# A chunked RWKV-7 recurrence with a SoLU layer behind it: small inverses transposed on VectorE, the first inverse moved, step 6 reordered

## The chip, the cores and the metric

The kernel runs on one core of a Trainium2 chip. The metric is the device time of one execution in microseconds. Before the change it is 708.82 us, the median of three runs (706.29 to 711.25). The profile is of one execution with a span of 705.0 us.

Engines are called PE (TensorE's matmuls; its weight loads are PEld), DVE (VectorE), ACT (ScalarE), POOL (GpSimd) and SP (SyncE, which here only issues transfers). [...]

## The reference

Inputs r, k, v, w, a, b have the shape (4 batches, 8 heads, 768 tokens, 40 channels), fp32. Each head carries a 40x40 state through time:

```
for t in range(768):
    y[t]  = r[t] @ state
    Sa    = state @ a[t]
    state = state * w[t] - outer(Sa, b[t]) + outer(v[t], k[t])
```

The outputs of the 8 heads, side by side, are rows x of 320 values, 3072 rows in all. The second layer computes

```
h    = x @ w_in                     # 320 x 1024
e    = exp(h - max(h)); solu = h * e / (sum(e) + 1e-9)
ln   = (solu - mean) / sqrt(var + 1e-6) * g_ln
out  = ln @ w_out                   # 1024 x 320
```

## The kernel before

**Chunks and steps.** Time is cut into 12 chunks ("rounds") of L = 64 tokens. A step handles one round of two of the four batches, so there are N = 24 steps; steps 2n and 2n+1 belong to round n. Within a chunk the recurrence becomes matrix products, except that the sequential term, the outer product of Sa and b, needs the inverse of a unit triangular 64x64 matrix for each head and batch. This inverse is built from inverses of its 32x32 blocks on the diagonal.

**The parts of a step** are Python generators; each `yield` ends a piece.

- `front(i)`: logarithm of w (lw, L352), its running sums on PE (pcum L356, pcx L369), scaled keys (kx), and the triangular matrix nt (L310). It runs five steps ahead (AHEAD = 5).
- `scatter(n)` writes the diagonal 32x32 blocks of round n to DRAM (blk_dram, L423), and `gather(n)` reads them back with one block to a partition (blk, L433 or L438).
- `invert(n)`: forward substitution on VectorE, one pair of small instructions to a piece. In rounds 0 to 3 (FINE = 4) only the 16x16 blocks are inverted so (L457, L459), in later rounds the whole 32x32 blocks (L492, L494). The result u goes to DRAM, and a transposed copy ut, made by VectorE or ScalarE (L466, L468, L498), goes there as well (L470, L501, L503).
- `bring_inverse(n)` fetches both from DRAM into the layout of the products: tinv from ut_dram (L512, L516) and tinvT from u_dram (L519).
- `solve(i)`: completes the inverses. In fine rounds two products join the 16x16 blocks (py16, y at L619, then pz16); in all rounds two more join the 32x32 blocks (py, pz). All products are groups of 32x32 matmuls at L567.
- Step 0 has no time to invert by substitution and builds its 16x16 inverses by doubling instead (L601 to L615). Each of three levels makes the product with the level's part (py2), y = 1 - product on DVE (L606), then both the new inverse (pz2) and its transpose (pu2) on PE, the one copied by ACT (L612), the other by DVE (L614).
- `attend(i)`, `recurrence(i)` and `readout(i)` are the rest of the attention; pu (L701) is the first product that uses the finished inverse, and x (L682) on DVE goes ahead of it.
- `hidden(m)` and `output(m)`: the second layer, six steps behind (LAG = 6).
- `weights()` fetches w_in and w_out, given as float64, piece by piece over POOL's queue and converts them on DVE and ACT (L178 to L190) during the first six steps. `centre()` (L267, L270) folds the mean of the layer norm into w_out at step 6.

**What sets the order.** Nothing is scheduled by a planner. The order of issue is written by hand as strings, one letter a piece: `turns("f g s ...")`, with EARLY for steps 0 to 5 and STEADY after that. `inverse_steps(i)` says how many pieces of `invert` each letter I runs. All SP transfers share one queue in program order[...]. "*" is a filler matmul without use (L872) that keeps PE active.

Before the change, the first inverse, that of step 1's blocks, runs at the end of the second `turns` (letters I with 2, 4, 4 and the rest), and the loads of rounds 1 and 2 are issued ahead of that `turns`:

```
load(1, "k")
load(1, "v")
load(2, "w")
load(1, "r")
load(2, "a", "b")
turns("f g s f s * g a s f s * f a s g s * g W a s I f s * f a I s a g I s * g f g I W W", ...)
load(2, "k")
scatter(1)
bring_inverse(0, slice(1, 2))
gather(1)
```

Of the kernel before, what the change touches and what calls it, by code (L numbers as in the profile page):

```python
# [64 lines left out]
def kernel(  # L65
# [26 lines left out]

    nc = tc.nc
# [61 lines left out]
    tn_t = const.tile([P, 2, H, 2, Q // 2], FP32, name="tinv")  # L155
# [37 lines left out]
    def weights():  # L193
# [3 lines left out]
        nc.sync.dma_start(out=g_rows, in_=moe_g_ln.rearrange("(c p) -> c p", p=P))  # L197
# [242 lines left out]
    def invert_fine(n):  # L440
# [4 lines left out]
        u = two.tile([P, R, Q], FP32, tag="u", name="u", bufs=1)  # L445
        ut = two.tile([P, R, Q], FP32, tag="ut", name="ut", bufs=1)
        nc.vector.tensor_scalar(out=x, in0=nb, scalar1=-1.0, scalar2=None, op0=ALU.mult)
        nc.vector.memset(x.rearrange("b c t -> b (c t)")[:, 0:R * R:R + 1], 1.0)
        for t in (u, ut):
            for z in range(2):  # L450
                nc.gpsimd.memset(t[half(z)][:, :, R * (1 - z):R * (2 - z)], 0.0)
# [9 lines left out]
        of_round[n]["spilt"] = u.rearrange("b c t -> b (c t)")  # L461
        for key, t, src in (("ut", ut, x.rearrange("b c t -> b t c")), ("u", u, x)):
            dst = of_round[n][key] = dram.tile([64, Q, Q], FP32, tag=key + "_dram", name=key + "_dram")
            for z in range(2):
                if n == 0 and key == "ut":
                    nc.vector.tensor_copy(out=t[half(z)][:, :, R * z:R * z + R], in_=src[half(z)])  # L466
                else:
                    nc.scalar.copy(out=t[half(z)][:, :, R * z:R * z + R], in_=src[half(z)])  # L468
            for z in range(2):
                nc.sync.dma_start(out=dst[:, R * z:R * z + R, :], in_=t[half(z)])  # L470
        yield

    def invert(n):
# [7 lines left out]
        u = two.tile([P, Q // 2, Q], FP32, tag="u", name="u", bufs=1)  # L481
# [15 lines left out]
        ut = two.tile([P, Q, Q // 2], FP32, tag="ut", name="ut", bufs=1)  # L497
        nc.vector.tensor_copy(out=ut, in_=u.rearrange("p c t -> p t c"))  # L498
        ut_dram = of_round[n]["ut"] = dram.tile([P, Q, Q // 2], FP32, tag="ut_dram", name="ut_dram")
        for p in range(2):  # L500
            nc.sync.dma_start(out=u_dram.rearrange("b (c z) t -> b c z t", z=2)[:, :, p], in_=u[half(p)])  # L501
            if p == 0:
                nc.sync.dma_start(out=ut_dram, in_=ut)  # L503
        yield

    def bring_inverse(n, steps=slice(0, 2)):

        ut, u = of_round[n]["ut"], of_round[n]["u"]
        tinv = tn_t[:, steps].rearrange("q s h z c -> q (s h) z c")
        for q in range(4):  # L510
            if n < FINE:
                nc.sync.dma_start(out=tinv[quarter(q)].rearrange("s h z c -> s h (z c)"),  # L512
                                  in_=ut[homes(q, steps)].rearrange("h s t -> s h t"))
            elif q % 2 == 0:
                for p in range(2):
                    nc.sync.dma_start(out=tinv[quarter(q), :, p],  # L516
                                      in_=ut[half(p)][homes(q)].rearrange("h s t -> s h t"))
# [34 lines left out]
    def solve(i):  # L552
# [3 lines left out]
        d["tinvT"], d["tinv"] = ti_t[:, i % 2], tn_t[:, i % 2]  # L556
        nt, tinv, tinvT = given(i, "nt"), d["tinv"], d["tinvT"]
# [16 lines left out]
        def whole(q):  # L574

            return (lambda p, g: nt[quarter(q), p, g, quarter(q % 2)],
                    lambda p, g: tinv[quarter(q), G * p + g].rearrange("s z c -> s (z c)"),
# [9 lines left out]
        if i == 0:  # L587
            tinv_rows, u_rows = tinv.rearrange("q h z c -> q h (z c)"), y_mid.rearrange("q p g c -> q (p g) c")
            unit = c_("one").unsqueeze(1).to_broadcast([P, H, Q])
            y = two.tile([P, H, Q], FP32, tag="u16", name="y", bufs=1)  # L590
# [13 lines left out]
            for j in range(1, 4):  # L604
                t = products("py2", each(level(j), lambda q: whole(q)[1]))
                nc.vector.tensor_tensor(out=y, in0=unit, in1=flat(t), op=ALU.subtract)  # L606
                if j == 1:
                    t = products("pu1", each(lambda q: whole(q)[1], eye))
                    nc.scalar.copy(out=u_rows, in_=flat(t))
# [249 lines left out]
    def inverse_steps(i):  # L859

        if i == 0:
            return [4, 4, 4, 4]
# [122 lines left out]
```

## Time and profile before

| | busy us | share of the span | instructions |
|---|---|---|---|
| PE | 630.7 | 89% | 12873 |
| PEld | 448.6 | 64% | 12873 |
| DVE | 438.4 | 62% | 1188 |
| ACT | 281.2 | 40% | 672 |
| POOL | 121.1 | 17% | 226 |

The shares are means over the whole span. PE counts each fp32 matmul as two records. The profile also slices the span into 40 equal parts and gives the busy share of each engine in a slice as a digit in tenths; PEclk is the clock that PE was granted, and DMA is the mean busy share of the 16 DMA engines. A stage's own limit is read from the slices and from busy time by stage. An entry such as "PE a <- DVE b: 8.2, 4, 3.3" says that PE stood idle ahead of a for 8.2 us in total, four times, 3.3 us the longest, and that DVE's instruction b ended it. "issue" means that the engine waited for nothing that the profile shows. A time line gives start and length of an instruction, and in square brackets the idle time ahead of it with what ended it.

Step 0's first pu (L701) starts at 59.88 us, step 1's at 94.86 us. From about 232 us on, a step takes 23.8 us.

### The profile page before, as it was taken

What the parts mean: (1) busy time and instruction counts of PE and PEld (TensorE: products, weight loads), DVE (VectorE), ACT (ScalarE), POOL (GpSimd) and SP (SyncE); (2) the same over time, 40 slices, a digit from 0 to 9 for tenths busy, and PEclk for the clock granted to TensorE, in tenths of its full rate; (3) what the DMA queues carried; (4) which work ended last, traced back from release to release, by engine and by line L of the source; (5) the groups of instructions that cost most, each with busy time, mean ns of one, the idle gap of its engine ahead of it and who ended that gap; (6) DMA issues with size and microseconds to landing.
All of it is one profiled execution on the core that took longest, in us unless ns stands there. A gap on an engine that the chain in (4) does not pass through costs nothing.

```text
span 705.0 us, 29268 instructions
## 1 busy us (share of the span) xinstructions
PE 630.7 (89%) x12873; PEld 448.6 (64%) x12873; DVE 438.4 (62%) x1188; ACT 281.2 (40%) x672; POOL 121.1 (17%) x226
## 2 busy tenths in 40 slices
PE   7677688898777999999999999999999899979996
PEld 4565566676655767766767676767666666545554
DVE  4116667558487578598697786876986753333442
ACT  3215255455651443444345334534352334312222
POOL 5401341233111112211221122112110100000000
PEclk9869869789997999999999999999999999998999
DMA  9853767568554455554456546554335230000000
GB/s 157 140 93 67 141 122 110 102 120 138 118 108 74 73 88 96 108 90 95 85 78 118 99 84 115 79 103 91 45 71 97 32 58 24 20 24 19 19 17 21
DMA packets 264254, 58.90 MB, mean 84 GB/s; under 512 B 251960, under 2 KB 259904, under 8 KB 264128
## 3 DMA queue, kind: packets, MB, share of 16 engines
q1 hardware_dynamic: 259056, 50.92, 42.6%
q0 software_dynamic: 1664, 5.24, 3.1%
q8 instruction: 101, 1.65, 1.0%
q10 hardware_dynamic: 3408, 0.87, 0.8%
q14 instruction: 25, 0.20, 0.1%
HBM read 38.92 MB, written 13.37 MB: 74 GB/s over the span
## 4 chain that ended last, share of the span: by engine, by line
PE 66%; DVE 15%; ACT 6%; issue 6%; DMA 3%; SPq 2%; ACTq 0%; POOL 0%; DVEq 0%
PE po L813 14%; PE h L768 13%; PE pyo L740 4%; PE plnT L808 4%; PE pcx L369 3%; DVE prod L492 3%; PE py L567 3%; DVE u L494 3%; PE pz L567 3%; PE pcum L356 2%; DVE nmax L778 2%; PE pyo L662 2%; PE plamv L307 2%; PE ppsi L307 2%; PE plamu L307 2%
## 5 line engine op out<-in xcount | busy, mean ns | idle before, releaser
L768 PE MATMUL h<-w_in,xT 128*128 128x512 f32 (+1 forms) x288 | 129.3, 640 | 3.9 <-DVE e L785 3.9
L813 PE MATMUL po<-w,lnT 128*128 128x320 f32 x384 | 115.0, 438 | 0.0
L813 PEld LDWEIGHTS po<-w,lnT 128*128 128x128 f32 x384 | 69.1, 191 | 26.4 <-issue 3.1
L494 DVE TENSOR_TENSOR u<-u,prod 128x30 f32<-128x30 f32 (+7 forms) x240 | 66.1, 275 | 8.2
L492 DVE TENSOR_TENSOR prod<-blk,u 128x30 f32<-128x30 f32 (+7 forms) x240 | 63.9, 266 | 8.2 <-DMA blk<-blk_dram 1.1
L359 POOL TENSOR_TENSOR kx<-raw_b,inv 128x320 f32<-128x320 f32 x24 | 20.8, 866 | 262.3 <-ACT inv L357 185.8
L778 DVE TENSOR_REDUCE nmax<-h 128x1 f32<-128x1024 f32 x24 | 29.3, 1221 | 47.4 <-PE h L768 47.4
L768 PEld LDWEIGHTS h<-w_in,xT 128*128 128x128 f32 (+1 forms) x288 | 38.5, 193 | 31.9 <-issue 30.0
L818 ACT ACTIVATE osb<-po,rs 128x320 f32<-128x320 f32 x24 | 12.7, 528 | 97.1 <-PE po L813 81.4
L747 DVE TENSOR_TENSOR x<-pyo,kx 128x512 f32<-128x512 f32 x24 | 16.6, 691 | 44.8 <-PE pyo L740 44.2
L809 ACT COPY lnT<-plnT 128x512 f32<-128x512 f32 x48 | 27.6, 587 | 35.7 <-PE plnT L808 35.6
L782 ACT ACTIVATE e<-h,nmax 128x1024 f32<-128x1024 f32 x24 | 26.8, 1116 | 35.0 <-DVE nmax L778 35.0
L800 POOL TENSOR_TENSOR rs<-c,mhalf 128x1 f32<-128x1 f32 x24 | 13.2, 550 | 156.7 <-DVE c L799 155.6
L785 DVE TENSOR_TENSOR e<-h,e 128x1024 f32<-128x1024 f32 x24 | 29.4, 1225 | 14.6 <-ACT e L782 14.0
L808 PE MATMUL plnT<-cst,e 128*128 128x128 f32 x192 | 30.5, 289 | 5.7 <-DVE e L785 5.4
L310 DVE TENSOR_TENSOR lamv<-plamv,cst 128x512 f32<-128x512 f32 x24 | 16.6, 691 | 30.3 <-PE plamv L307 30.1
L369 PEld LDWEIGHTS pcx<-cst,lw 128*128 128x128 f32 x192 | 28.2, 202 | 9.7 <-ACT y_mid L646 3.6
L369 PE MATMUL pcx<-cst,lw 128*128 128x132 f32 x192 | 33.3, 301 | 1.1 <-ACT kx L371 0.5
L650 ACT ACTIVATE tinvT<-pz 32x256 f32<-32x256 f32 x48 | 17.9, 374 | 39.9 <-PE pz L567 39.6
L371 ACT ACTIVATE kx<-pcx 128x264 f32<-128x264 f32 x48 | 18.9, 393 | 35.0 <-PE pcx L369 33.0
L808 PEld LDWEIGHTS plnT<-cst,e 128*128 128x128 f32 x192 | 22.9, 146 | 14.2 <-issue 4.3
L726 POOL TENSOR_TENSOR sm<-tot,fac 128x320 f32<-128x320 f32 x20 | 14.7, 736 | 98.2 <-DVE tot L725 71.6
(144 smaller groups left out, 1221.0 us busy)
## 6 DMA issues: line engine op xcount, KB each, us to landing
blk<-blk_dram SPq DMA_DIRECT2D x16, 256.0 KB
raw_k<-in_k_dram SPq DMA_DIRECT2D x24, 160.0 KB
v<-in_v_dram SPq DMA_DIRECT2D x24, 160.0 KB
r<-in_r_dram SPq DMA_DIRECT2D x24, 160.0 KB
out_dram<-osb SPq DMA_DIRECT2D x24, 160.0 KB
raw_w<-in_w_dram SPq DMA_DIRECT2D x23, 160.0 KB
raw_b<-in_b_dram SPq DMA_DIRECT2D x23, 160.0 KB
raw_a<-in_a_dram SPq DMA_DIRECT2D x23, 160.0 KB
```

Source lines behind the costliest of these rows:

```text
L307: nc.tensor.matmul(t[half(c ^ p * cross), p, g * L:(g + 1) * L], lhsT=lhs[half(p), g, half(c)], rhs=rhs[half(p), g, half(c)], start=True, ...
L369: nc.tensor.matmul(t[:, g * 132:g * 132 + 132], lhsT=pair(lw, 2 * j + g), rhs=cst[:, lo:lo + 132], start=True, stop=True)
L492: nc.vector.tensor_tensor(out=t, in0=nb[:, j:j + 1, j + 1:Q].to_broadcast([P, rows, m]), in1=u[:, 0:rows, j:j + 1].to_broadcast([P, rows, ...
L494: nc.vector.tensor_tensor(out=u[:, 0:rows, j + 1:Q], in0=u[:, 0:rows, j + 1:Q], in1=t, op=ALU.subtract)
L567: nc.tensor.matmul(t[quarter(out), c:c + Q], lhsT=lhs(p, g), rhs=rhs(p, g), start=True, stop=True)
L740: nc.tensor.matmul(t[half(p), c, g * W:g * W + used], lhsT=kb[half(c), j, 2 * g + p, :], rhs=lam[half(c), h % 2, h // 2, 0:used], start=i ...
L768: nc.tensor.matmul(h[:, j * 512:j * 512 + 512], lhsT=of_round[i // 2]["xT"][rows, kt, i % 2 * P:i % 2 * P + P], rhs=w_in[rows, 4 if kt == ...
L778: nc.vector.tensor_reduce(out=nmax, in_=h, axis=AX.X, op=ALU.max, negate=True)
L785: nc.vector.tensor_tensor(out=q, in0=h, in1=e, op=ALU.mult)
L808: nc.tensor.transpose(out=t[:, j * P:(j + 1) * P], in_=q[:, f * P:(f + 1) * P], identity=ident)
L809: nc.scalar.copy(out=lnT[:, fs.start:fs.stop].rearrange("p f t -> p (f t)"), in_=t)
L813: nc.tensor.matmul(o[:, 0:DM], lhsT=lnT[:, f, :], rhs=w2[:, f, :], start=f == 0, stop=f == NF - 1)
```

## The change

ut is no longer made, stored and fetched. Instead VectorE transposes tinvT's 32x32 blocks in place of the fetch of tinv: one new piece at the head of `solve(i)` for i > 0, for which the strings EARLY, STEADY and CENTRE have one more "s" right behind the last "r", some pieces ahead of the first product. In step 0 VectorE's transposes take the place of the products pu, pu2 and of half of pz16. The first inverse is spread among step 0's doublings, and the loads of round 2 (w, a, b) and of round 1 (v, r) are issued behind it. Step 6 has an order of its own, and the inversion pieces of the early steps are distributed anew.

```diff
-    tn_t = const.tile([P, 2, H, 2, Q // 2], FP32, name="tinv")
+    tinv = const.tile([P, 2, G, L], FP32, name="tinv")
...
-        nc.sync.dma_start(out=g_rows, in_=moe_g_ln.rearrange("(c p) -> c p", p=P))
+        nc.gpsimd.dma_start(out=g_rows, in_=moe_g_ln.rearrange("(c p) -> c p", p=P))
...
-        u = two.tile([P, R, Q], FP32, tag="u", name="u", bufs=1)
-        ut = two.tile([P, R, Q], FP32, tag="ut", name="ut", bufs=1)
+        u = two.tile([P, R, Q], FP32, tag="u", name="u")
...
-        ut = two.tile([P, Q, Q // 2], FP32, tag="ut", name="ut", bufs=1)
-        nc.vector.tensor_copy(out=ut, in_=u.rearrange("p c t -> p t c"))
-        ut_dram = of_round[n]["ut"] = dram.tile([P, Q, Q // 2], FP32, tag="ut_dram", name="ut_dram")
...
-                nc.sync.dma_start(out=tinv[quarter(q)].rearrange("s h z c -> s h (z c)"),
-                                  in_=ut[homes(q, steps)].rearrange("h s t -> s h t"))
...
             t = products("py1", each(level(0), eye))
-            nc.vector.tensor_tensor(out=tinv_rows, in0=unit, in1=flat(t), op=ALU.subtract)
+            nc.vector.tensor_tensor(out=t_0, in0=unit, in1=flat(t), op=ALU.subtract)
+            nc.vector.transpose(out=u_0, in_=t_0)
             yield
             for j in range(1, 4):
                 t = products("py2", each(level(j), lambda q: whole(q)[1]))
                 nc.vector.tensor_tensor(out=y, in0=unit, in1=flat(t), op=ALU.subtract)
-                if j == 1:
-                    t = products("pu1", each(lambda q: whole(q)[1], eye))
-                    nc.scalar.copy(out=u_rows, in_=flat(t))
                 yield
                 t = products("pz2", each(lambda q: whole(q)[2], grown))
-                nc.scalar.copy(out=tinv_rows, in_=flat(t))
-                t = products("pu2", each(grown, lambda q: whole(q)[2]))
-                nc.vector.tensor_copy(out=u_rows, in_=flat(t))
+                nc.scalar.copy(out=t_0, in_=flat(t))
+                nc.vector.transpose(out=u_0, in_=t_0)
                 yield
+        else:
+            cols = slice(0, L if fine else Q)
+            nc.vector.transpose(out=tinv[:, :, :, cols], in_=tinvT[:, :, :, cols])
+            yield
...
-                         [(q, whole(q)[2], whole(q)[3]) for q in (0, 2)])
+                         [(q, whole(q)[2], whole(q)[3]) for q in (0, 2) if i])
...
-    EARLY = ("r r a r B W f I r r W I W y r X W a s f L W a I a s W f a f W s I a f W s I f W",
-             "r r a r W f r r W g W y r W a f g L W a I a s f g W a I s f g W I s a f g W I s f g W")
-    STEADY = "r b r a r B f b b o r o I o r o y o r X I o h a f L a s a h f a I h f s h f h a f h"
+    EARLY = ("r r a r B W f I r r W I W y r s X W a I s f L W a I a s W f I a f W s I a f W s f W",
+             "r r a r W f r r W g W y r s W a f g L W a I a s f g W a I s f g W I s a f g W I s f g W I")
+    STEADY = "r b r a r B f b b o r o I o r o y o r s X I o h a f L a s a h f a I h f s h f h a f h"
+    CENTRE = "r r a r f o I r o r o y o r s X I o h a f L a s a h I f s a h I f s h f s h I a f h"
...
         if i == 0:
-            return [4, 4, 4, 4]
+            return [4, 4, 4, 3, 1]
         if i == LAG - 1:
-            return [0, 0, 4, 5, 5]
+            return [0, 0, 4, 4, 3, 3]
+        if i == LAG:
+            return [3, 3, 4, 4, 4]
         if i < LAG:
-            return [0, 0, 2, 3, 3] if i % 2 else [3, 3, 1, 1, 0]
+            return [0, 0, 2, 2, 2, 2] if i % 2 else [3, 3, 1, 1, 0, 0]
...
-        load(1, "v")
-        load(2, "w")
-        load(1, "r")
-        load(2, "a", "b")
-        turns("f g s f s * g a s f s * f a s g s * g W a s I f s * f a I s a g I s * g f g I W W",
-              dict(I=[2, 4, 4, 99]), f=f, g=g, s=so, a=at, I=inv, W=ws, **{"*": warmer})
+        turns("f g s f s * g a s f I s I f a s I g I s I g a I", dict(I=[2, 3, 3, 3, 3, 99]), f=f, g=g, s=so, a=at, I=inv,
+              **{"*": warmer})
+        bring_inverse(0, slice(1, 2))
+        load(2, "w", "a", "b")
+        turns("s f W s * f a s a g s g f g W W", {}, f=f, g=g, s=so, a=at, W=ws, **{"*": warmer})
+        scatter(1)
         load(2, "k")
-        scatter(1)
-        bring_inverse(0, slice(1, 2))
         gather(1)
+        load(1, "v", "r")
```

Where step 6 took STEADY with some letters moved, it now takes CENTRE. In steps below 6 the last pieces of an inverse come earlier in the step than before.

## The prediction

> **What bounds the kernel now.** I read the page's slices first, then busy time by stage, then the list of what the matmul engine waited for, then the time line around the longest of these waits.
>
> The slices (PE busy, its granted clock, the DMA engines, each in tenths, 17.6 us a slice):
>
> ```profile
> PE   7677688898777999999999999999999899979996
> PEclk9869869789997999999999999999999999998999
> DMA  9853767568554455554456546554335230000000
> ```
>
> PE is at 9 from the fourteenth slice on and at 6 to 8 before it. So the kernel has a matmul-bound part, and a first third in which the in-order PE stands still a quarter of the time. By stage (each pair is busy us and instructions; then clock and DMA share):
>
> ```profile
> 15.00:59.00 44.00, 31.74 (x1168) 25.65 (x1170) 12.38 (x37) 12.25 (x29) 11.14 (x19) 0.81 0.68 104
> 59.00:110.00 51.00, 37.70 (x917) 29.84 (x906) 33.60 (x102) 23.12 (x60) 16.26 (x32) 0.77 0.67 123
> 110.00:215.00 105.00, 85.93 (x2678) 69.46 (x2676) 70.24 (x225) 59.20 (x163) 25.49 (x47) 0.92 0.65 115
> 232.00:550.00 318.00, 309.22 (x6128) 219.46 (x6129) 238.71 (x636) 132.54 (x308) 50.10 (x88) 1.00 0.51 90
> ```
>
> From 232 to 550 us PE lacks 8.8 of 318 us: nothing to win there. From 15 to 232 us it lacks 49. What it waited for (total, times, longest), over the whole run:
>
> ```profile
> PE pu L701 <- DVE x L682: 8.2, 4, 3.3
> PE pz L567 <- issue: 5.7, 3, 4.0
> PE py L567 <- issue: 5.4, 3, 2.8
> ...
> PE pcum L356 <- ACT lw L352: 5.0, 2, 4.1
> PE pu L567 <- issue: 4.4, 2, 2.8
> PE pz L567 <- DVE y L619: 3.9, 1, 3.9
> ```
>
> And single waits in the time line (start, length, instruction, idle time before it), PE's and then VectorE's:
>
> ```profile
> 33.24 0.47 PE L567 MATMUL pu<-y_mid,y 32*32 32x32 f32 x34 [2.80 <-issue]
> ...
> 40.26 0.26 PE L567 MATMUL py<-tinv,level 32*32 32x32 f32 x8 [2.80 <-issue]
> ...
> 64.69 1.44 PE L356 MATMUL pcum<-lw,cst 128*128 128x320 f32 x2 [4.06 <-ACT lw L352]
> ...
> 81.86 1.08 PE L567 MATMUL pz<-tinvT,y 32*32 32x32 f32 x64 [3.99 <-issue]
> ```
>
> ```profile
> 79.88 0.29 DVE L447 TENSOR_SCALAR u<-blk 128x256 f32<-128x256 f32 x1 [4.35 <-DMA blk<-blk_dram]
> ```
>
> The "issue" waits break off in the middle of a run of small matmuls (34 of 64 left), so no operand is missing. Five of them, 8.5 us, lie between 23 and 45 us, where the DMA share in windows of 5 us is 0.8 to 1.25; from 45 to 60 us it is 0.01 to 0.03 and there is none. I take them as instruction blocks that arrive late behind the loads of rounds 1 and 2. The 3.99 us at 81.86 I read otherwise: its operand y (L619) was written at 81.41, queued on VectorE behind the first inversion piece (L447) that waited 4.35 us for its blocks.
>
> [...] an fp32 two-operand op[...] here 128x256 shows 0.42 and 128x512 0.69 us[...]. [...] the clock was 0.50 from 45 to 50 us and again from 85 to 95, each time behind several long waits.
>
> **The change, part by part.**
>
> *Price of a transpose.* The trace shows none. [...] 0.42 us for 128x256 and 0.69 for 128x512 (estimate). [...]
>
> *Step 0's doublings (L601 to L615).* PE loses pu (32 products once, 1.08 us), pu2 (three times 0.75, 0.90, 1.36: 3.0) and half of pz16 (0.68): 144 products, 4.8 us. Three of five warmers go: 0.8, 1.0, 0.6: 2.4. Together 7.2 us, all on PE's path, since PE is busy or starved there nearly without a gap. Four transposes take the place of three copies on VectorE (12.4 of 44 us busy): hidden beside the next py, which needs only ScalarE's copy.
>
> *Order of loads.* Before 24 us nothing changes. Then the queue held v1, w2, r1, a2, b2 (26 to 43 us); now only k1 stays ahead of the first inverse, and the weights start later too. Of 8.5 us of issue waits I expect 2.5 to remain: 6.0 saved. Against it, the first inversion piece now waits on VectorE for its blocks ahead of a transpose, and the chain py, y, pz, copy, transpose becomes visible: +2. This stage: -11.2, the first pu (L701) at about 48.7 us instead of 59.9.
>
> *First inverse.* It ended at 62.1, after the solve, and ScalarE's copy of it (L468) stood ahead of lw (L352): PE's 4.06 us. Now it ends some 8 us before the solve; its copy is ahead of the solve's own copies and waits for nothing. lw then waits for w2, whose load is issued behind the inverse: inverse at 39.3, copy 40.2, store and bring to 45, w2 issued by 47, landed by 50; lw is due at 49. Saved 4.06 less 1.5: 2.5.
>
> *Blocks of round 1.* In the queue: w2, a2, b2 to 51, scatter to 53.5, k2, gather to 57, landed at 61 (4 us, as 75.9 to 79.9). The piece that needs them comes at 60. The wait of 4.35 shrinks to 1 or 2, and y with it: of 3.99 I take 2.
>
> *Transposed store and fetch.* 16 ut stores, 48 fetches, 16 copies go; SyncE's queue is 3 us shorter per round and the packets fall by some 23,500 (48 fetches, most of 512 short rows). Steady steps: tinvT's fetch moves up to 335.3 to 337.3, lands by 340.9 (3.5 us, as 101.6 to 105.1), VectorE reaches the transpose at 342.9, PE needs it at 346.8. Queued behind it are inversion pieces and psi, with 25% of VectorE free; the sum update on GpSimd is ahead of it. VectorE gains 17 transposes (7.1 us) and 7 wide ones (4.8) against 8 copies of 0.61: no PE time. In the early odd steps the transpose may wait for the fetch up to 1 us; py waited 2.8 us in all for tinv: -0.5 net, +2 held for new waits of this kind.
>
> *Where the inversion pieces stand.* In steps 1, 3 and 5 a piece group right ahead of nt and x (L682) delayed pu: 2.6, 1.0 and 3.35 us. It moves earlier: saved 1.5 of the first two and 2.5 of the last. In step 6, 13 of 18 pieces preceded y (L619): now 6, two to four us sooner, against a stall of 3.94: saved 2.
>
> *Nothing:* g_rows on another queue (first used at 121 us), a second buffer of u, fewer GpSimd memsets (2.5 us on an engine busy 17%).
>
> Sum: -11.2 - 2.5 - 2 - 0.5 + 2 - 1.5 - 2.5 - 2 = -20.2, from 708.8 to about 689.
>
> **Rivals.**
> 1. *The starvation moves with the loads.* w2 to r1 now fall on the end of the solve and on step 0, which also crosses many small matmuls. For it: every early window with share above 0.8 has such waits. Against: from 60 to 86 us only one short one (0.75 us) is left once the 3.99 is read as above. Then half of the load order's gain goes (3), lw waits (2.5) and the blocks come late (2), and 1 more: -20.2 + 8.5 = -11.7, 697 to 702 with its own spread.
> 2. *VectorE becomes the gate (slower).* It executes in order; a transpose that waits for tinvT holds everything behind it. For it: the fetch's slack is only 2 us in steady steps, and the price is unseen. If fetches land 4 us later than I think and transposes cost twice: 8 odd steps by 2.5 and 9 even ones by 0.9 make +28 against -20: 717. Against: blocks fetched behind tinvT were waited for only about 1 us a round at 343.8.
> 3. *Given back.* The early steps compress onto VectorE, which also has the weights' conversion (70 of 105 us from 110 to 215); saved waits reappear as pu <- x. About 707.
>
> **How the numbers follow.** Forecast 0.70, rival 1 0.15, rival 2 0.08, rival 3 0.07. The forecast's own spread is 680 to 697: all issue waits of that stage gone and waits of steps 5 and 6 gone whole gives 680. Up to 703 takes in rival 1; rivals 2 and 3 and the lowest end are left out. Faster by over 1% (below 701.7): 0.70 and two thirds of rival 1, 0.80. Slower: rival 2, 0.08. Within 1%: 0.12.
>
> **What would show it.** Right: first pu (L701) at 47 to 52 us; issue waits between 23 and 45 us under 3 us; no wait of pcum for lw over 2 us; transposes at 0.4 and 0.7 us; 232 to 550's step of 23.8 us unchanged; waits of pu for x under 4 us in all. Wrong: a transpose idle for a DMA in most odd steps, PE waits for y or tinv after it, new issue waits from 50 to 75 us, or a longer steady step.

## The result, and the profile after

The changed kernel takes 684.24 us, the median of 4 runs (682.73 to 685.31), against 710.04 us before (706.29 to 711.8): ratio 0.9642, interval 0.9596 to 0.9688. A second set of 6 runs beside 9 of the kernel before gave 682.6 us, ratio 0.9620, interval 0.9575 to 0.9665. Three of the 29 executions of the kernel before that ran beside the experiments were slow ones (714.8 to 716.0 us) and are left out of every comparison. 689.0 was forecast, with 680 to 703 as the range. The profiled spans are 681.7 us, and 705.0 us before; the changed kernel has a second profile, of 680.5 us, from experiment 9, which stands beside the first wherever one profile could mislead.

The slices after, 17.0 us each:

```profile
PE   7678777887888999999999999999998999979996
PEclk9998778996999999999999999999999999989999
DMA  9559857474362356545444543554234020000000
```

DMA has moved: 5 in the second slice where it had 8, and 9 in the fourth where it had 3, which are the loads of rounds 1 and 2. PE's nines begin with the fourteenth slice as before, of slices that are now shorter. By stage (the columns as before: PE, PEld, DVE, ACT and POOL with busy us and instructions, then clock, DMA share, GB/s):

```profile
15.00:46.90 31.90, 23.39 (x893) 18.77 (x892) 17.22 (x50) 11.94 (x28) 11.09 (x18) 0.95 0.57 102
46.90:97.00 50.10, 35.58 (x941) 28.79 (x941) 33.64 (x100) 23.20 (x63) 15.47 (x28) 0.76 0.77 137
97.00:196.00 99.00, 82.11 (x2533) 65.83 (x2536) 67.73 (x214) 52.78 (x147) 23.47 (x43) 0.90 0.59 106
212.00:530.00 318.00, 309.20 (x6167) 219.92 (x6167) 243.87 (x656) 133.10 (x308) 50.95 (x89) 1.00 0.46 82
```

Step 0's stage, from 15 us to its first pu, is 31.9 us long instead of 44.9 (35.1 in the second profile), with some 290 matmuls fewer and as many weight loads. The steady stretch has the same PE busy time as before, 309.20 and 309.22 us. What PE waited for:

```profile
PE py L547 <- DVE tinv L598: 11.3, 5, 6.4
...
PE pcum L357 <- ACT lw L353: 4.9, 2, 3.7
...
PE pu L684 <- DVE x L665: 3.1, 3, 1.6
...
PE pz L547 <- DVE tinv L589: 2.8, 1, 2.8
PE pz L547 <- DVE y L602: 2.4, 2, 1.4
PE py L547 <- issue: 2.2, 2, 2.0
...
PE pz L547 <- issue: 1.8, 2, 1.4
```

The waits of pz, py and pu for "issue" were 15.5 us in the lines of before, with the 3.99 us of pz that the prediction reads otherwise. Now they are 2.2 us for py, 1.8 for pz and none for pu; in the second profile 1.5, 5.4 and none. A new one, py for the transposed inverse (L598 is VectorE's transpose), has the first place, with 11.3 us (12.2 in the second profile). Single waits in PE's time line, one of VectorE's, and the transposes among VectorE's groups:

```profile
20.55 0.37 PE L547 MATMUL py<-tinv,level 32*32 32x32 f32 x18 [2.01 <-issue]
29.02 0.34 PE L308 MATMUL ppsi<-kx,kT 64*64 64x64 f32 x6 [1.24 <-issue]
...
33.52 1.07 PE L547 MATMUL pz<-tinv,y_mid 32*32 32x32 f32 x64 [2.82 <-DVE tinv L589]
...
51.35 1.44 PE L357 MATMUL pcum<-lw,cst 128*128 128x320 f32 x2 [3.73 <-ACT lw L353]
...
89.01 1.08 PE L547 MATMUL py<-tinv,nt 32*32 32x32 f32 x64 [6.43 <-DVE tinv L598]
```

```profile
28.84 0.30 DVE L447 TENSOR_SCALAR u<-blk 128x256 f32<-128x256 f32 x1 [3.16 <-DMA blk<-blk_dram]
```

```profile
L598 DVE STREAM_TRANSPOSE tinv<-tinvT 128x256 f32<-128x256 f32 x16 | 7.0, 434 | 0.0
L598 DVE STREAM_TRANSPOSE tinv<-tinvT 128x512 f32<-128x512 f32 x7 | 4.9, 703 | 4.7 <-DMA tinvT<-u_dram 4.7
```

Of 23 transposes ahead of py one waited for its fetch, 4.7 us in step 1, and that one makes the 6.43 us on PE. The other four waits of py for tinv, 0.8 to 1.3 us each, are not for a fetch: VectorE was busy with other pieces ahead of the transpose.

**Where the 23.3 us went.** PE busy fell from 630.7 to 613.8 us, 16.9, and its idle time from 74.3 to 67.9, 6.4. Busy time holds two things, which the mean granted clocks, 0.945 and 0.960, allow to estimate: busy times clock is 596.0 and 589.2, so some 6.8 us is work that is gone and some 10.1 us is work that ran faster. By place, with a step counted from its first pu to the next one's (us):

| | before | after | after, second profile |
|---|---|---|---|
| up to step 0's pu | 59.9 | 46.9 | 50.1 |
| step 0 | 35.0 | 29.9 | 24.2 |
| step 1 | 25.5 | 27.0 | 28.4 |
| step 2 | 25.8 | 21.6 | 24.3 |
| step 3 | 20.3 | 21.1 | 21.4 |
| step 4 | 21.5 | 27.1 | 25.8 |
| step 5 | 22.0 | 22.4 | 21.7 |
| step 6 | 29.1 | 23.6 | 23.7 |
| step 7 to the end | 466.0 | 462.3 | 460.9 |

Step 4 lost what others won. PE has the same matmuls there as before, but two issue waits of 1.42 and 1.80 us (one of 1.19 before), and the clock, 1.00 before, is 0.75, so that PE is busy 22.3 us where it was busy 17.1:

```profile
146.30:173.40 27.10, 22.31 (x587) 18.11 (x586) 14.48 (x48) 12.59 (x35) 5.70 (x10) 0.75 0.58 104
```

### The profile page after: what moved, and what is told of

Same layout as the page of the kernel before. It is cut to its first block, busy times and chain, and to the rows that moved or that the text cites. A ratio compares the mean times of both kernels' runs of the same rounds, so it can differ in the third digit from the quotient of the medians.

```text
span 681.7 us, 28591 instructions
## 1 busy us (share of the span) xinstructions
PE 613.8 (90%) x12579; PEld 435.1 (64%) x12579; DVE 446.8 (66%) x1203; ACT 276.5 (41%) x663; POOL 119.9 (18%) x219
## 4 chain that ended last, share of the span: by engine, by line
PE 67%; DVE 16%; ACT 5%; issue 5%; DMA 4%; SPq 2%; ACTq 0%; DVEq 0%
PE po L796 15%; PE h L751 13%; PE pyo L723 5%; PE plnT L791 4%; PE pcum L357 3%; PE pcx L370 3%; PE pz L547 3%; PE py L547 2%; DVE prod L486 2%; DVE u L488 2%; DVE nmax L761 2%; PE plamv L308 2%; PE pyo L645 2%; PE plamu L308 2%; PE ppsi L308 2%
## 5 line engine op out<-in xcount | busy, mean ns | idle before, releaser
L751 PE MATMUL h<-w_in,xT 128*128 128x512 f32 (+1 forms) x288 | 127.7, 633 | 3.9 <-issue 3.9
L486 DVE TENSOR_TENSOR prod<-blk,u 128x30 f32<-128x30 f32 (+7 forms) x240 | 66.1, 275 | 7.3 <-DMA blk<-blk_dram 0.4
L488 DVE TENSOR_TENSOR u<-u,prod 128x30 f32<-128x30 f32 (+7 forms) x240 | 64.5, 269 | 8.2
L547 PE MATMUL py<-tinv,nt 32*32 32x32 f32 x1280 | 23.7, 197 | 12.6 <-DVE tinv L598 11.3
L791 PE MATMUL plnT<-cst,e 128*128 128x128 f32 x192 | 29.5, 282 | 5.7 <-DVE e L768 5.4
L370 PEld LDWEIGHTS pcx<-cst,lw 128*128 128x128 f32 x192 | 27.1, 197 | 10.7 <-ACT y_mid L629 3.4
L547 PEld LDWEIGHTS py<-tinv,nt 32*32 32x32 f32 x1280 | 20.3, 111 | 17.7 <-issue 13.4
```

Source lines behind the costliest of these rows:

```text
L370: nc.tensor.matmul(t[:, g * 132:g * 132 + 132], lhsT=pair(lw, 2 * j + g), rhs=cst[:, lo:lo + 132], start=True, stop=True)
L486: nc.vector.tensor_tensor(out=t, in0=nb[:, j:j + 1, j + 1:Q].to_broadcast([P, rows, m]), in1=u[:, 0:rows, j:j + 1].to_broadcast([P, rows, ...
L488: nc.vector.tensor_tensor(out=u[:, 0:rows, j + 1:Q], in0=u[:, 0:rows, j + 1:Q], in1=t, op=ALU.subtract)
L547: nc.tensor.matmul(t[quarter(out), c:c + Q], lhsT=lhs(p, g), rhs=rhs(p, g), start=True, stop=True)
L751: nc.tensor.matmul(h[:, j * 512:j * 512 + 512], lhsT=of_round[i // 2]["xT"][rows, kt, i % 2 * P:i % 2 * P + P], rhs=w_in[rows, 4 if kt == ...
L791: nc.tensor.transpose(out=t[:, j * P:(j + 1) * P], in_=q[:, f * P:(f + 1) * P], identity=ident)
```

## The experiments

Differences between kernels are taken from their ratios to the kernel before, times 709 us; for the changed kernel the mean of its two ratios, 0.9631, is used. The intervals have half widths of 0.4 to 0.6%, so such a difference is uncertain by 4 to 5 us. What is said of single waits and of a first pu rests on one profile of each kernel, two of the changed one.

**1. The inversion pieces and step 6 as before, the rest changed.**

```diff
-    EARLY = ("... y r s X W a I s f L W a I a s W f I a f W s I a f W s f W", ...
+    EARLY = ("... y r s X W a s f L W a I a s W f a f W s I a f W s I f W", ...
...
-            turns(CENTRE if i == LAG else order, dict(I=inverse_steps(i)), **parts)
+            if i == LAG:
+                order = order.replace("a s a h f a I h f s h f h", "a s a h f s a I h f s h f s h")
+            turns(order, dict(I=inverse_steps(i)), **parts)
```

> The changed kernel with the old places of the inversion pieces: old counts in steps 0 to 6, old strings but for the new transposing piece, old order of step 6. My theory: the waits of pu for x at the starts of steps 2 and 6 and of pz for y in step 6 come back (1.5, 2.5 and 2 us by the prediction), so 688 to 691 us instead of 684, and the first pu of step 0 stays at 46.9 us. Rival, that the places of the pieces do nothing and the whole gain is made before step 1: 684 within 1 us and no wait of pu for x over 2 us.

Measured: 687.1 us, ratio 0.9712 (0.9657 to 0.9767). Step 6 takes 29.9 us, against 23.6 in the changed kernel, and its waits are back (total, times, longest):

```profile
PE py L547 <- DVE tinv L598: 3.4, 1, 3.4
PE pz L547 <- DVE y L602: 2.3, 1, 2.3
PE pu L684 <- DVE x L665: 2.0, 1, 2.0
```

So the new places are worth 5.7 us, uncertain by 4.5, and the waits say why: in step 6 pieces stood ahead of tinv, y and x in VectorE's queue.

**2 and 3. The loads of rounds 1 and 2 early again; or w of round 2 alone.**

```diff
         load(1, "k")
+        load(1, "v")
+        load(2, "w")
+        load(1, "r")
+        load(2, "a", "b")
         turns("f g s f s * g a s f I s I f a s I g I s I g a I", ...
         bring_inverse(0, slice(1, 2))
-        load(2, "w", "a", "b")
...
-        load(1, "v", "r")
```

> The changed kernel with the loads of rounds 1 and 2 (v, w, r, a, b) issued ahead of the turns again, as in the kernel before. My theory (small matmuls starve for instructions behind the loads): the issue waits between 22 and 47 us come back from 1.2 us to 5 to 8 us and the first pu moves from 46.9 to 51 to 54 us; the first inverse reaches memory later, lw no longer waits for w (3.7 us saved) and the fetch in step 1 is no longer behind v and r (some of its 6.4 us saved); the whole 683 to 690. Rival (starvation is no matter of the loads, only fewer products count): the first pu stays at 47 us, and with both later waits saved the whole is 675 to 679.

Measured: 682.45 us, ratio 0.9652 (0.9596 to 0.9708), in total the same as the changed kernel. The first pu did move, to where the first theory had it:

```profile
52.40 1.19 PE L684 MATMUL pu<-tinvT,x 64*64 64x64 f32 x32
```

In the changed kernel it comes at 46.87 and 50.14. The issue waits between 23 and 45 us grew less than that theory asked for, to 3.1 us (1.2 and 3.1 in the changed kernel), and the clock in that window is 0.73 (0.92 and 0.81). PE doesn't wait for lw in step 0 now, and by step 2's pu the kernels are level: 103.8, against 103.7 and 102.7. In the third experiment, only w moves ahead:

```diff
         load(1, "k")
+        load(2, "w")
...
-        load(2, "w", "a", "b")
+        load(2, "a", "b")
```

> The changed kernel with round 2's w alone issued ahead of the turns, behind k of round 1. My theory: lw no longer waits for its data, so the 3.7 us of pcum for lw in step 0 go; two transfers bring at most one issue wait of 1 to 2 us; the step 1 fetch still comes too late and takes back part. 681 to 684. Rival (what is saved ahead of step 1 is lost again to the fetch of tinvT behind the queue): 684 within 0.7 us, with the wait of py for the transpose in step 1 longer by what was saved.

Measured: 681.45 us, ratio 0.9625 (0.9585 to 0.9665), also the same. The wait of pcum for lw fell from 3.73 to 0.8 us without a gain that can be told; the changed kernel's second profile shows 1.0 us there with no edit at all. So one profile can't tell how far the order of the loads decides this wait. It doesn't decide the total.

**4. Step 0's products back on PE, everything else changed.**

```diff
             nc.vector.tensor_tensor(out=t_0, in0=unit, in1=flat(t), op=ALU.subtract)
-            nc.vector.transpose(out=u_0, in_=t_0)
...
+                if j == 1:
+                    t = products("pu1", each(lambda q: whole(q)[1], eye))
+                    nc.scalar.copy(out=u_0, in_=flat(t))
...
-                nc.vector.transpose(out=u_0, in_=t_0)
+                t = products("pu2", each(grown, lambda q: whole(q)[2]))
+                nc.vector.tensor_copy(out=u_0, in_=flat(t))
```

> The changed kernel with step 0's transposes by PE products again (pu, three times pu2, half of pz16) and their copies, 144 small products, all else as changed. My theory: they lie on PE's path, 4.8 us at the old clock, some 4 at full clock, plus at most one issue wait: first pu at 51 to 53 us instead of 46.9, the whole 687 to 690. Rival (the doublings are bound by the chain through VectorE and ScalarE, PE has room): first pu at 47 to 48 us and the whole within 1 us of 684.

Measured: 686.71 us, ratio 0.9682 (0.9627 to 0.9737): 3.6 us slower than the changed kernel, within the uncertainty of 4.5. Its first pu comes at 55.1 us, against 46.9 and 50.1 in the two profiles of the changed kernel. The issue waits are back, though the loads are late. PE's time line:

```profile
24.21 0.48 PE L547 MATMUL pz<-tinv,y_mid 32*32 32x32 f32 x19 [1.29 <-issue]
...
32.48 0.47 PE L547 MATMUL pu<-y_mid,tinv 32*32 32x32 f32 x34 [1.36 <-issue]
...
35.92 0.26 PE L547 MATMUL py<-tinv,level 32*32 32x32 f32 x6 [1.06 <-issue]
...
41.84 0.42 PE L547 MATMUL pu<-y_mid,tinv 32*32 32x32 f32 x11 [3.33 <-issue]
```

For other engines PE waits little here, 1.3 us in all from 23 us to the first pu. With experiment 2 this makes a square. Issue waits of PE that end between 23 and 45 us, the DMA share there, and the first pu:

| | loads early | loads late |
|---|---|---|
| products on PE | before: 8.5 us, share 0.97, pu 59.9 | experiment 4: 7.0 us, share 0.38, pu 55.1 |
| transposes on DVE | experiment 2: 3.1 us, share 0.93, pu 52.4 | changed: 1.2 us (3.1 in its second profile), share 0.47, pu 46.9 (50.1) |

The loads move the waits by 2 us at most. With late loads the products bring 4 to 6 us of them. The left column is no clean pair, because experiment 2 differs from the kernel before also in the order of the work (first inverse, warmers); experiment 8 comes back to it. Cutting the profile of before at the instants of its issue waits shows what they are:

```profile
20.30:24.28 3.98, 3.50 (x127) 2.46 (x128) 0.42 (x1) 0.81 (x2) 0.62 (x1) 0.58 0.86 125
24.28:28.41 4.13, 3.02 (x127) 2.40 (x127) 0.42 (x1) 1.39 (x3) 1.89 (x4) 1.00 0.78 111
28.41:33.24 4.83, 2.03 (x129) 1.75 (x129) 0.42 (x1) 0.76 (x2) 3.43 (x6) 1.00 0.93 150
33.24:40.26 7.02, 4.22 (x128) 3.54 (x128) 1.12 (x2) 0.39 (x1) 2.30 (x7) 0.76 1.17 200
40.26:44.81 4.55, 2.97 (x128) 2.56 (x128) 0.42 (x1) 0.76 (x2) 0.00 (x0) 0.55 0.85 124
```

From one wait to the next, PE runs 127 to 129 matmuls and as many weight loads: some 256 instructions, each time, whatever they are. In experiments 4, 7 and 8 and in the changed kernel's second profile the waits of this stage lie as far apart, 127 to 129 matmuls, or twice that, 254 to 256. In the profile of before the instruction queue q8 moved 101 packets, 1.65 MB, so 16.3 KB each, and one of them in each of these five stretches; PE's 25,746 matmuls and weight loads make 255 to a packet. I read the waits, an estimate from these figures, as waits for the next block of some 256 instructions; the trace doesn't name what PE waited for. Here 256 instructions are 2.0 to 4.2 us of matmuls. A group of 32 products is 64 matmuls and 64 weight loads, half a block, so the 144 removed products were 576 instructions, 2.25 blocks.

**5. The scatter of the blocks behind the fetch of tinvT.** It aims at the 6.43 us of step 1, where the scatter (3.5 us of issuing) stands between the store of the inverse and its fetch.

```diff
         bring_inverse(n)
+        if i < LAG and i + AHEAD - 1 < N:
+            scatter((i + AHEAD - 1) // 2)
...
-            if js and js[-1] % 2:
+            if js and js[-1] % 2 and i >= LAG:
                 scatter(js[-1] // 2)
```

> The changed kernel with one move in SyncE's queue: in the first six steps the scatter of the next blocks is issued behind the fetch of tinvT instead of ahead of it. Theory A (the fetch of tinvT is late in step 1 because the scatter, about 3.5 us of issuing, stands between the store of the inverse and the fetch): the fetch is issued about 3.5 us sooner, VectorE's transpose no longer waits 4.7 us for it, PE's wait of py for tinv in step 1 falls from 6.4 us to 3 or less, and the whole kernel gains 1 to 3 us, 681 to 683. Theory B (the fetch is held by the store of the inverse or by the solve's own reads of the other tinvT, not by the scatter): the wait stays above 5 us and the time stays within 1 us of 684. If the blocks then come later and the pieces wait for them, a wait of VectorE for blk of some us appears and the gain is given back.

Measured: 693.54 us, ratio 0.9797 (0.9754 to 0.9841): some 12 us slower than the changed kernel. The fetch was issued 3.3 us sooner (80.19 instead of 83.49 us), but tinvT landed only 1.7 us sooner, and the wait is 5.73 us. The blocks came late in three steps. VectorE's time line, first pieces of an inverse:

```profile
91.80 0.29 DVE L447 TENSOR_SCALAR u<-blk 128x256 f32<-128x256 f32 x1 [4.22 <-DMA blk<-blk_dram]
...
142.67 0.29 DVE L447 TENSOR_SCALAR u<-blk 128x256 f32<-128x256 f32 x1 [4.33 <-DMA blk<-blk_dram]
...
191.06 0.42 DVE L476 TENSOR_SCALAR u<-blk 64x512 f32<-64x512 f32 x1 [3.83 <-DMA blk<-blk_dram]
```

and PE's:

```profile
143.75 1.08 PE L547 MATMUL pz<-tinvT,y 32*32 32x32 f32 x64 [2.96 <-issue]
...
194.18 1.08 PE L547 MATMUL pz<-tinvT,y 32*32 32x32 f32 x64 [5.39 <-issue]
```

Here "issue" stands ahead of the first of all 64 records of pz, not in the middle of a group: y (L602) was written at 143.30 and 193.73, behind those pieces on VectorE. This is the wait of 3.99 us at 81.86 in the kernel before, brought about by one edit. Both pz run at 1.08 us instead of 0.7, and so does what follows.

**6. Five fillers in place of the products.** A filler (128x256, two PE records and no operand to wait for) after y of the first doubling level, after each y-pz pair and after pz16.

```diff
+                if j == 1:
+                    next(warmer)
                 yield
...
                 nc.scalar.copy(out=t_0, in_=flat(t))
+                next(warmer)
                 nc.vector.transpose(out=u_0, in_=t_0)
...
+            if i == 0:
+                next(warmer)
```

> The changed kernel with five filler matmuls of 128x256 (the kernel's own warming instruction, about 0.6 to 0.9 us each, 3.5 to 4 us in all) at the places in step 0 where the products pu, pu2 and half of pz16 stood. PE has nearly the removed products' time back, in 10 instructions instead of 144. Theory A (the removed products cost more than their own time: with so many instructions the array waits for instructions): issue waits before the first pu stay at 3 us or less, the first pu comes 1 to 4 us later than in the changed kernel and well before the 55.1 us of the kernel with the products back, time 684 to 687. Theory B (the products' own time is what counted): first pu at 53 to 56 us, as with the products back, time 686 to 689.

Measured: 679.97 us, ratio 0.9621 (0.9582 to 0.9660): no slower than the changed kernel, and below both forecasts. First pu at 45.0 us; issue waits before it 1.74, 0.49, 0.71 and 0.23. The stage:

```profile
15.00:45.00 30.00, 24.26 (x903) 19.56 (x901) 16.57 (x50) 11.96 (x28) 11.12 (x18) 1.00 0.60 110
```

PE does more and is done no later, at full clock. Given back in 20 instructions (10 matmuls, 10 weight loads), PE's time costs nothing that can be told; given back in 576, it comes with 7.0 us of issue waits and a first pu at 55.1 us. So the products' own time does not show as a cost. That it is free isn't shown: the clock is also higher with the fillers, 1.00 here against 0.95 and 0.85 in the changed kernel, and they may pay for themselves that way.

**7 and 8. The later transposes alone, then with those of step 0.** The seventh is the kernel before with this part changed, and with g_rows on POOL's queue and the second buffer of u, which the prediction put at nothing:

```diff
-        ut = two.tile([P, Q, Q // 2], FP32, tag="ut", name="ut", bufs=1)
-        nc.vector.tensor_copy(out=ut, in_=u.rearrange("p c t -> p t c"))
...
-                nc.sync.dma_start(out=tinv[quarter(q)].rearrange("s h z c -> s h (z c)"),
-                                  in_=ut[homes(q, steps)].rearrange("h s t -> s h t"))
...
+            nc.vector.transpose(out=tinv[:, :, :, cols], in_=tinvT[:, :, :, cols])
```

> The kernel before with one part of the change: in the steps above 0 the transposed inverse is made on VectorE out of tinvT instead of being stored transposed and fetched. Step 0, the order of loads and the places of the inversion pieces are the old ones. Theory A (this part is worth nothing by itself, since the stores and fetches were hidden and the transposes are hidden now): 705 to 711, ratio within 0.5% of 1, and a longer wait of py for tinv in step 1, 2 to 6 us. Theory B (the freed queue and the fewer packets are a good part of the gain): below 702. Theory C (VectorE's transposes are in the way where the pieces stand at their old places): above 712.

Measured: 699.61 us, ratio 0.9885 (0.9841 to 0.9929). This part is not neutral: it gives about 8 us, uncertain by 3, in the range of theory B. SyncE's queue before and in this kernel, in the same place (start, time to issue):

```profile
69.20 3.26 SPq L512 DMA_DIRECT2D tinv<-ut_dram  x4
72.51 2.04 SPq L519 DMA_DIRECT2D tinvT<-u_dram  x4
74.60 1.31 SPq L433 DMA_DIRECT2D blk<-blk_dram  x2
```

```profile
69.27 1.92 SPq L499 DMA_DIRECT2D tinvT<-u_dram  x4
71.36 2.29 SPq L434 DMA_DIRECT2D blk<-blk_dram  x2
```

Without the tinv fetch the blocks of round 1 are asked for 3.2 us sooner, the first piece no longer waits 4.35 us for them, and of pz's 3.99 us 0.63 is left. Step 0, from its pu to the next, takes 29.5 us instead of 35.0. Against this stand a first pu 1.3 us later, a new wait of py for tinv, 5.2 us in step 1, and step 6 at 31.0 instead of 29.1. Both profiles reach step 7's pu at the same time (238.9 and 239.0), and behind it this kernel is 4.9 us shorter. But 3.1 us of that come and go between executions of the same code. Step 20 takes 23.4 us in the kernel before and 21.8 here; in the two profiles of the changed kernel it takes

```profile
525.40:548.80 23.40, 21.84 (x410) 15.03 (x411) 17.21 (x49) 8.36 (x19) 1.86 (x4) 0.93 0.23 36
```

```profile
525.90:547.70 21.80, 20.26 (x410) 13.72 (x410) 17.12 (x49) 8.35 (x19) 1.87 (x4) 1.00 0.21 39
```

The end, from step 23's pu, takes 92.3 us in the kernel before and 90.8 here; in experiments 2 and 6, whose code there is that of the changed kernel, it takes 92.3 and 92.2, and in the changed kernel 90.8 and 90.7. So the profiles show where a local wait went, but hardly any of the 8 us. Over its runs this kernel's clock is 0.955 on average, that of the 9 runs of before beside it 0.944. What raises it is open.

The eighth adds the transposes of step 0 to the seventh:

```diff
+            nc.vector.transpose(out=u_0, in_=t_0)
...
-                t = products("pu2", each(grown, lambda q: whole(q)[2]))
-                nc.vector.tensor_copy(out=u_0, in_=flat(t))
```

> The kernel with the later transposes alone and, on top, the four transposes of step 0 in place of pu, pu2 and half of pz16; five warmers, the old order of loads and the old places of the pieces stay. Theory A (the products with the waits for instructions that go with them are the largest part of the first stage's gain): 6 to 10 us below the kernel with the later transposes alone, the first pu 6 to 9 us sooner, issue waits before it down from about 10 to under 5 us. Theory B (the early loads and the place of the first inverse are what makes the waits): issue waits stay at 7 us or more and the gain is at most the products' own 4.8 us.

Measured: 692.54 us, ratio 0.9804 (0.9751 to 0.9856), 5.7 us below the seventh, between the two forecasts and uncertain by 5. First pu at 53.5 us instead of 61.2, but issue waits before it only from 11.0 to 8.6 us. So theory A holds in the first pu and theory B in the waits: in the old order of this stage two blocks still come 2.9 and 2.3 us late, where experiment 2, with the same loads as early but the new order of the work between them, waits 5.1 us in all. With early loads, then, taking the products away saves 2.4 us of these waits and the new order of the work 3.5. How the inverse's pieces and the warmers share in that was not taken apart further.

**9. The changed kernel again, and without its two warmers.**

> The changed kernel itself once more, for a second profile and a second interval beside the three others of this group. Both theories: 684 within 2, ratio 0.960 to 0.969. If the stall costs are set by the kernel (theory A), the waits of its second profile are those of the first within 1 us each (py for tinv 6 to 7 us in step 1, pcum for lw 3 to 4); if they are chance (theory B), the waits move about and only the sum agrees. The clock of the first stage is expected to differ from the first profile's 0.95.

Measured: 682.6 us, ratio 0.9620 (0.9575 to 0.9665). py's wait for tinv in step 1 is 6.64 us again; pcum's for lw is 1.0 instead of 3.73; first pu 50.1 instead of 46.9, at clock 0.85 instead of 0.95; step 7's pu is at 219.6 instead of 219.4. Single waits of the first 80 us are partly chance; by step 7 the two profiles agree.

```diff
-        turns("f g s f s * g a s f I s I f a s I g I s I g a I", ...
+        turns("f g s f s g a s f I s I f a s I g I s I g a I", ...
...
-        turns("s f W s * f a s a g s g f g W W", ...
+        turns("s f W s f a s a g s g f g W W", ...
```

> The changed kernel without the two warming matmuls that it still has in step 0, so none where the kernel before has five and the kernel with fillers seven. Theory A (a warming matmul costs its own time, 0.6 to 1 us, as the prediction had it): 1 to 2 us faster, 682 to 683. Theory B (it pays more than it costs, because it fills waits and the array's clock does not fall to half): slower by 1 to 6 us, 685 to 690, with a lower clock in the first stage.

Measured: 682.99 us, ratio 0.9619 (0.9574 to 0.9664), the same. The clock of the stage up to the first pu (at 48.8 us) is lower, 0.76, as theory B had it, but the loss it forecast isn't there. With none, two or seven fillers the kernel takes the same time within what can be told.

**10. Earlier w and fillers together.**

```diff
+        load(2, "w")
...
+                next(warmer)
```

> The changed kernel with the two edits that were faster by themselves: round 2's w is loaded ahead of step 0, and five filler matmuls stand where step 0's products were. Theory A (the two gains, 2 to 3 us for the earlier w and about 3 us for the clock, lie in different stages and add up): 676 to 679. Theory B (both act through the granted clock of the same stretch, or are given back at the wait of step 1 for tinv): 680 to 682. In either case the wait of pcum for lw is under 1.5 us and issue waits before the first pu under 3 us.

Measured: 682.47 us, ratio 0.9629 (0.9580 to 0.9678): no gain to be told, which is theory B's forecast.

**11. And step 1's wait filled, steps 2 and 4 transposed first.** Six more fillers stand ahead of the py of step 1 that waits for tinv.

```diff
+            if i == 1:
+                order = order.replace("W a I s f L", "W a I * * * * * * s f L")
+                parts["*"] = idlers()
+            if i in (2, 4):
+                order = "s " + order.replace(" s X", " X")
```

> The kernel with the earlier w and the fillers, and on top six more filler matmuls in step 1 right ahead of py, where PE waits some 6 us for tinv, and VectorE's transpose at the head of steps 2 and 4 instead of right ahead of its use. Theory A (such a wait costs a second time, because the clock is at half for some 10 us behind it): the wait of py in step 1 shrinks by the fillers' 4 us without py coming later, the clock of that step is above 0.85, and the whole is 2 to 5 us below the kernel without this, of which the transposes give 1 to 2 us (the waits of py for tinv in steps 2 and 4, 1.3 and 0.8, go under 0.3). Theory B (the clock recovers by itself and fillers only stand in the way): within 1 us of the kernel without this, or slower.

Measured: 675.94 us (673.66 to 681.46), ratio 0.9538 (0.9482 to 0.9593), the fastest of all: 6.7 us below the changed kernel on the same chip and 6.5 below experiment 10. The mean clock over its runs is 0.970, against 0.959 for the changed kernel. Its profiled execution is the slowest of its six (span 679.5), so it shows the gain only in part. In step 1 py still waited 4.35 us, 2.3 less than in the changed kernel's second profile. In step 4, the changed kernel (second profile) and this one:

```profile
148.40:174.20 25.80, 20.36 (x591) 16.10 (x590) 13.85 (x45) 12.47 (x35) 5.72 (x10) 0.87 0.61 104
```

```profile
149.90:170.70 20.80, 17.60 (x590) 14.26 (x590) 13.77 (x46) 12.13 (x34) 5.80 (x10) 1.00 0.74 127
```

The same work, 2.2 us less idle time and 2.8 us less busy time at full clock. This gives back what step 4 had lost: it took 21.5 us before the change. Which of the two edits did it is open: the added instructions also shift where each stretch of some 256 instructions ends. They weren't run apart.

## Why the prediction was right, and where its reasons were not

The total lies inside the range and 5 to 6 us below the forecast. In part this is luck: two of the terms had the wrong size, in opposite directions. The parts by ratio, each kernel against the one before it, in us of 709: later transposes 8.2; transposes of step 0 5.7; first inverse, order of loads and fewer warmers (experiment 8 to 1) 6.5; places of pieces and step 6 5.7. Each of these differences carries an uncertainty of 3 to 5 us, and the kernels are from different sets of runs. Point by point:

- **Step 0's stage, -11.2.** The first pu was forecast at 48.7 and came at 46.9 and 50.1: the sum holds. The step "instruction blocks that arrive late behind the loads of rounds 1 and 2" fits the trace in the blocks (254 to 258 instructions from wait to wait before) and hardly in the loads, which move these waits by 2 us at most. The waits fell by 7.3 and 5.4 us, near the 6.0 booked on the order of loads, but what took them away is the missing products and the new order of the work. Early loads do put the first pu off, by 2.3 to 5.5 us, at a lower clock, and the total doesn't change (experiment 2). The 4.8 us of the products' own time are not shown as a cost (experiment 6), and the 2.4 booked for three warmers was nothing that can be told (experiment 9). The +2 for a piece that waits for its blocks ahead of a transpose was right in mechanism: VectorE waited 3.16 us and PE behind it 2.82 us. In the second profile VectorE's wait is missing.
- **lw, -2.5.** 0.3 us in one profile, 3.1 in the other. The sign "no wait of pcum for lw over 2 us" failed in the first (3.73) and held in the second (0.95), and the total is the same when w comes early (experiment 3). ScalarE's lw waited 2.67 us for w in the first profile and not at all in the second, so whether w lands in time differs between executions.
- **Blocks of round 1, -2.** The reading of 3.99 us as y behind a waiting piece was right, and 3.1 us of it went (3.99 to 0.92). Experiment 7 shows that the shorter queue is enough for that, and experiment 5 brings the same wait about.
- **Transposed store and fetch, -0.5 + 2.** The term with the largest error: forecast +1.5, measured -8.2. The waits for tinv were under-sized too (2 forecast; 2.8 became 11.3, with 6.4 in one step, a sign of being wrong that the prediction had named). The earlier blocks, already booked above, outweigh a part of them. The rest of the gain goes with a higher clock, and its cause is open.
- **Places of pieces, -6.** 5.7 by the total; step 6 alone is 6.3 us shorter than in experiment 1, and pu waited 3.1 us for x in all, under the 4 forecast.
- **Transposes.** 434 and 703 ns against the 420 and 690 estimated, which is what VectorE's two-operand instructions of the same size take in the profile of before (y L606 421 ns, x L747 691 ns). Between the two sizes each further element of a partition costs 1.05 ns. In the steady steps the transposes delayed nothing (23.8 and 23.7 us, as before).
- **Not booked: step 4.** It became 4.3 to 5.6 us longer, by issue waits and the half clock behind them.

The prediction counted 13 us of waits, net, beside 7.2 us of PE time. The profiles show 6.8 us of work, 6.4 us of idle time, and 10.1 us of granted clock, which it had left at nothing. Over all runs it is the same: the kernel before lost 5.8% of the clock on average over the 26 runs beside the experiments (clocks 0.933 to 0.954), the changed one 4.2% over its 10. In the traces shown here a low clock stands behind waits (0.50 behind py's 6.64 us in step 1, 0.51 behind 1.42 and 1.80 us in step 4); no run changes the clock alone, so what each removed wait was worth in clock stays an estimate.

Of the rivals, the first (starvation moves with the loads) fell: between 50 and 75 us, where it expected new waits, the changed kernel has one issue wait of 1.14 us (1.15 in the second profile), and putting the loads back leaves the total as it is. The second had its mechanism in one step, the transpose that waits 4.7 us for its fetch, and not its size. The third is seen in part: experiments 2 and 3 shorten the wait for lw of the first profile and the total does not follow, and step 4 gave back 4.3 to 5.6 us, though not as waits for x.

## What to carry to other kernels

Count instructions as well as microseconds where matmuls are small: in this stage 256 of them were 2 to 4 us of PE time, and what taking 576 away visibly saved was issue waits (7.0 us with them, 1.2 and 3.1 without), not their own time. A transfer that looks hidden can hold those behind it in its queue (without the fetch of tinv the blocks were asked for 3.2 us sooner), and what comes late there can stand in an engine's queue ahead of something urgent (pz's 3.99 us before, 0.63 in experiment 7). Cost a wait together with the matmuls at half clock behind it (9.4 us at 0.50 behind py's 6.64). And profile a kernel twice before explaining a difference of a few us: here two profiles of the same code differ by 3 us in the first pu and by 6 us in the step behind it.

## What the runs showed of the hardware

- The half clock outlasted the wait ahead of it. In the second profile of the changed kernel, PE's time line behind the wait of step 1:

```profile
86.87 1.07 PE L547 MATMUL py<-tinv,nt 32*32 32x32 f32 x64 [6.64 <-DVE tinv L598]
...
95.26 1.11 PE L400 MATMUL paT<-cst,a 128*128 128x128 f32 x4
96.31 0.76 PE L547 MATMUL py<-tinv,nt 32*32 32x32 f32 x32
```

  PE works without a gap from 86.87 us and is at full speed only from 96.3, 9.4 us later; the granted clock in between is 0.50. In step 4 of the first profile, behind waits of 1.42 and 1.80 us, it is 0.51 for 10.1 us of work without a gap (163.3 to 173.4). In experiment 11 the half clock ends 4.3 us after the wait of 4.35 us. So the work without a gap before full speed took 4.3 to 10.1 us in these three places.
- The places in the instruction stream where PE waits for "issue" stay the same, some 256 instructions apart, and the length of the wait varies. With 12 matmuls of the last pu of step 0's doublings left it is 1.58 us in the kernel before and 3.08 in experiment 7, with 11 left 3.33 in experiment 4. In the two profiles of the changed kernel, with 11 of pz left, it is 0 and 1.04 us.
- A VectorE transpose of 32x32 blocks took 434 ns for 128x256 and 703 ns for 128x512 elements of fp32.
